# Block-sparse attention and SwiGLU: batch 1 moves from dense attention to attention by blocks

## The chip, the core and the metric

The kernel runs on one core of a Trainium2 chip. The metric is the device time of one execution in microseconds (us). The engines of the core are written as the profile writes them: PE is the matrix engine (PEld its weight loads), DVE the vector engine, ACT the scalar engine, POOL the GpSimd engine, and SP the engine that here only issues DMAs. A DMA can be issued from the queue of SP, ACT or POOL; the profile writes SPq, ACTq and POOLq for such a queue. PSUM is the memory that PE writes, in eight banks; SBUF is the memory that all engines read and write.

## What is computed

Four batches of attention with eight heads, 768 tokens and 64 elements per head, then a feed-forward part over the 3072 rows of 512 elements that come out. Tokens lie in 24 blocks of 32. A block of queries sees its own block and the two beside it, the first and the last block, and three sampled blocks; the first and the last block see everything.

```python
    scores = scale * np.matmul(q, k.transpose(0, 1, 3, 2))
    mask = np.abs(blk_i - blk_j) <= window
    mask = mask | (blk_i == 0) | (blk_j == 0) | (blk_i == n_blocks - 1) | (blk_j == n_blocks - 1)
    for qb in range(n_blocks):
        for kb in sampled_blocks[qb]:
            mask[qb * block:(qb + 1) * block, kb * block:(kb + 1) * block] = True
    scores = np.where(mask, scores, -1000000000.0)
    attn = softmax(scores)                      # written out in the reference
    x = np.matmul(attn, v)                      # (B, H, S, D) -> rows (B * S, H * D)
    xn = x / np.sqrt(np.mean(x * x, axis=-1, keepdims=True) + 1e-06) * rms_g
    g = xn @ w_gate
    out = (g / (1 + np.exp(-g)) * (xn @ w_val)) @ w_out
```

## The kernel before

**Units.** The work is cut into units (`UNITS`): a batch, the tiles of 128 tokens that the unit takes, and how many they are (1 to 3). A unit is attention for its tiles, a normalization, and the feed-forward part for them. Batch 0 has units of 1, 1, 1 and 3 tiles, batches 1 to 3 two units of 3 tiles each.

**Dense batches (0 and 1; `NDB = 2`).** Scores are computed for all pairs of tokens; the mask enters as 24 more rows of the contraction. `dk` (L322) makes scores of 128 keys by the unit's queries, `dexp` (L343) the exponentials on ACT, `dav` (L357) multiplies with the values, and `dxo` (L369, L370) divides. Tokens are dealt to partitions with a step of six (`(p c)`), so a load reads 1536 bytes in a row. Keys and queries of batch 0 are turned on PE (`tpx`, L301). Those of batch 1 are cast by `fill` into AUG and turned by a DMA transpose on SP (`turn`, L288).

**Batches by blocks (2 and 3).** Only the seen blocks are computed, four query blocks to a tile. `load_kv` and `load_q` (L452, L459) load, `fill_k`, `fill_q` and `fill_v` cast to bf16, `turn_k` and `turn_q` (L478, L504) turn keys and queries by DMA. `kg_fixed` copies the key blocks that do not depend on the data, `kg_sampled` those at sampled blocks, whose offset is in a register (both end in the helper `copy`, L144 to L148). Values are written to HBM as rows of all heads (`store_v`, L508) and gathered from there: `pair_v` (L570 to L578) what is fixed, `block_v` (L555) the sampled blocks, one DMA of 32 rows for each. `block_v` issues sampled blocks 0 and 1 from SP and block 2 from ACT. `qk` (L599), `exp` (L605), `av` (L648) and `xo` (L658, L659) do the attention; tile 5 holds the first, the last and two more blocks, whose scores are made by `qka` (L615) and `expa` (L623). Tokens are dealt in pairs (`(t p c)` with c = 2), so k and v are read 512 bytes in a row, q 256, and the turned keys hold even and odd tokens apart.

**Feed-forward.** `sq`, `rsq` and `xq` (L672 to L693) normalize. For the first six units (`NPET = 6`) xn is turned on PE (`tr`, L704) and copied out by `cp`; for the others by a DMA transpose (`xt`, L715). `proj` (L728) makes the gate part in bank 4 and the value part in bank 5, `th` (L737) takes a tanh of the gate part on ACT, `uu` (L743) and `hp` (L754) multiply on DVE. Bank 4 is free for the next gate part after `uu`. `yy` (L767) is the last matmul, `yo` (L777, L779) the copy out, `so` the store.

**Order.** No engine's order is written by hand. Every step is an `op` with the engines that may do it, an estimated duration, the steps it waits for, a priority, and the buffers or banks it takes and gives back. The loop at the end of the kernel takes, again and again, the step that can start earliest by these estimates, with priority as the tie-break, and records it; so the estimates and due times (`at`, such as `IXAT` and `RGAT`) set the order in which each engine's queue is filled. On the chip each queue runs in that order. First loads have an order of their own (`seq`). `gate_sync` is a small DMA from a loaded weight on SP, which makes the loads after it wait until that part of the weights has come.

**Registers.** The sampled blocks are read into registers by `table_regs` (L435), on POOL for key offsets and on SP and ACT for value offsets.

Of the kernel before, what the change touches and what calls it, by code (L numbers as in the profile page):

```python
# [16 lines left out]
def kernel(  # L17
# [32 lines left out]
    NR, NHP, NXN, NYO, NPET = NRND, 2, 2, 3, 6  # L50
    NSLOT, NAUG, NOPEN, NDB = 5, 2, 2, 2
    IXAT, RGAT = 36.0, 48.0
    NPT, NPA, NKG, NVG, NRAW = 4, 2, 2, 3, 3
    AHEAD, HURRY, HURU = 0.8, ("av", "xo", "sq", "rsq", "xq", "tr", "cp"), 0
# [3 lines left out]
    HD = NC * D // 2  # L58
    UNITS = [(0, 0, 1), (0, 1, 1), (0, 2, 1), (0, 3, 3)]
    UNITS += [(b, c, 3) for b in range(1, NDB) for c in (0, 3)]  # L60
    ND = len(UNITS)
    for b in range(NDB, B):
        UNITS += [(b, (5, 0, 1), 3), (b, (2, 3, 4), 3)]
    NU = len(UNITS)
    HG = [("h", 0 if u < 3 else u) for u in range(NU)]
    HO = [u if u < 3 else 0 for u in range(NU)]
# [9 lines left out]
    def bank16(n):  # L76
# [12 lines left out]
    VAC = const.tile([P, 2, H * NC, D + 2], BF16, name="VAC")  # L89
    VGC = const.tile([P, 6, VW], BF16, name="VGC")  # L90
# [6 lines left out]
    RAWD = list(A)  # L97
    RAWS = [RAWC[:, i * RB:(i + 1) * RB] for i in range(NRAW)]
    aug = [AUG[:, i] for i in range(NAUG)]
    va_ = [VAC[:, i] for i in range(2)]  # L100
    vfl = [t.rearrange("p m d -> p (m d)")[:, 0:6 * VW] for t in va_]
    VAUG = [t.rearrange("p (t c h d) -> p t c h d", t=NC // 2, c=2, h=H) for t in (vfl[0], PTC[:, 10240:10240 + 6 * VW])]
    rt_ = RAWC[:, NRAW * RB:].bitcast(BF16)
    VGB = [VGC, rt_[:, 0:6 * VW].rearrange("p (x w) -> p x w", w=VW),
           vfl[1].rearrange("p (x w) -> p x w", w=VW)]
    PD = [PTC[:, i * PDW:(i + 1) * PDW] for i in range(3)]
    PTB = [t.rearrange("p (h l x) -> p h l x", h=2, l=2) for t in [rt_[:, 6 * VW:6 * VW + 1024]] + [
        PTC[:, i * 1024:(i + 1) * 1024] for i in range(NPT - 1)]]
    PAB = [PTC[:, 3072 + i * 2048:3072 + (i + 1) * 2048].rearrange("p (l h x) -> p l h x", l=2, h=2) for i in range(NPA)]
    KTB = [t.rearrange("p (a s) -> p a s", a=NP) for t in (xs_[3], xs_[1])]  # L110
    QTB = [t.rearrange("p (a s) -> p a s", a=NP) for t in (xs_[4], PTC[:, 7168:7168 + NP * S])]
    KGB = [xs_[i].rearrange("p (x a s j c) -> p x a s j c", x=6, a=NP, s=4, j=16) for i in (0, 2)]
    KROW = AUG[:, 0].rearrange("p i e c x -> p (i e c x)").rearrange(
        "p (a c t x) -> p a c t x", a=NP, c=2, t=NC // 2)
    QROW = AUG[:, 1].rearrange("p i e c x -> p (i e c x)").rearrange("p (a n x) -> p a n x", a=NP, n=NC)
    kvv = [t.rearrange("b h (t p c) d -> b p (h t) (c d)", p=P, c=2) for t in (k, v)]
    qvv = q.rearrange("b h (n p) d -> b n p h d", p=P)
# [32 lines left out]
    zt = const.tile([P, VW], BF16, name="zt")  # L150
# [36 lines left out]
    nc.gpsimd.memset(zt[0:32, P:VW], 0.0)  # L187
# [9 lines left out]
    for t in va_:  # L197
        nc.vector.memset(t[:, :, D:D + 1], 1.0)
# [72 lines left out]
    def load(g, i):  # L271
        b, pr = divmod(g, NP)
        if i == 0:
            rawd[g] = RAWD[held["rawd", g][1]]
        nc.sync.dma_start(out=rawd[g][:, i], in_=(kv, qv, vv)[i][b, :, 2 * pr:2 * pr + 2, :])

    def fill(g, i, eng):
        copy(eng, aug[g % NAUG][:, i, :, :, 0:D],
             rawd[g][:, i].rearrange("p h (c d) -> p h c d", d=D))

    def pad_v(g, eng):
        b, pr = divmod(g, NP)
        src = rawd.pop(g) if b else A[g]
        copy(eng, va_[b][:, 2 * pr * NC:2 * (pr + 1) * NC, 0:D],
             src[:, 2].rearrange("p h (c d) -> p (h c) d", d=D))

    def turn(g):
        nc.sync.dma_start_transpose(  # L288
            out=X[g % NSLOT].rearrange("p i e (c t) -> p (i e c) t", t=P),
            in_=aug[g % NAUG].rearrange("p i e c r -> p (i e c r)"))  # L290

    def zero_pad(i):
        nc.vector.memset(aug[i][:, :, :, :, KQ:P], 0.0)
# [15 lines left out]
    held, rawd = {}, {}  # L309
# [38 lines left out]
    def dav(u, pr, bk):  # L348
        b, c0, nt = UNITS[u]
        pt, va = pts.pop((u, pr)), va_[b]  # L350
        o_ = PS[:, bk[0], 0:nt * 2 * (D + 1)].rearrange(
            "p (t e d) -> p t e d", t=nt, e=2)
        tiles["o", u, pr] = o_
        for t in range(nt):
            for e in range(2):
                for jt in range(NC):
                    nc.tensor.matmul(  # L357
                        out=o_[:, t, e, :], lhsT=pt[:, jt, e, t * P:(t + 1) * P],
                        rhs=va[:, (2 * pr + e) * NC + jt, 0:D + 1],
                        start=(jt == 0), stop=(jt == NC - 1))  # L360
# [14 lines left out]
    tab_, at_ = VGB[0].rearrange("p x w -> p (x w)"), [0]  # L375

    def small(n, dt, p=P):
# [7 lines left out]
    kti, vti = small(NS * 2, I32, 1), small(NS * NR, I32, 1)  # L385
    koff, voff = {}, {}

    REGS = {"POOL": [("k", 0, 16), ("k", 16, 32), ("k", 32, 2 * NS)], "SP": [("v", 0, 16), ("v", 16, 32), ("v", 32, 2 * NS)],
            "ACT": [("v", 2 * NS, 2 * NS + 11), ("v", 2 * NS + 11, 3 * NS)]}
    HALF = 1024  # L390

    def load_table():
        nc.sync.dma_start(
            out=stab.rearrange("p n r i -> p (n r i)"), in_=s64.rearrange("n x -> (n x)").unsqueeze(0))
        for b in range(NDB, B):
            for lo in (0, S + 32):
                nc.sync.dma_start(out=vrows[b][lo:lo + 32, :], in_=zt[0:32, :])

    def table(i, eng):
# [3 lines left out]
        elif i == 1:  # L403
            TC(out=sf, in_=stab[:, 1:NB - 1, :, 0])
            TS(out=d2, in0=sf, scalar1=16.0, scalar2=None, op0=ALU.mult)
# [17 lines left out]
        else:  # L423
# [4 lines left out]
            TS(out=vti.rearrange("p (r n) -> p n r", r=NR), in0=d2, scalar1=32.0, scalar2=32.0, op0=ALU.mult, op1=ALU.add)  # L428
# [3 lines left out]
    def table_regs(eng, part):  # L432
        e = {"POOL": nc.gpsimd, "ACT": nc.scalar, "SP": nc.sync}[eng]
        w, lo, hi = REGS[eng][part]
        _, got_ = nc.values_load_multi_w_load_instructions(  # L435
            {"k": kti, "v": vti}[w][0:1, lo:hi], engines=[e.engine], min_val=0,
            max_val={"k": 16 * (NB - 1) * (HALF + 1), "v": 32 * (NB + 1)}[w], skip_runtime_bounds_check_because=WHY)
        for i_, x in enumerate(got_):
            r, n = divmod(lo + i_, NS)
            {"k": koff, "v": voff}[w][n * NR + r] = x  # L440

    def k_at(n, r):
        x = koff[n * NR + min(r, 1)]
        if r:
            x = x >> 10 if r == 2 else x & (HALF - 1)
        return nc.s_assert_within(x, 0, 16 * (NB - 1), skip_runtime_bounds_check_because=WHY)


    def load_kv(b, i, hf):
        key = ("kv"[i], b, hf)  # L450
        raws[key] = RAWS[held["raw", key][1]]
        nc.sync.dma_start(  # L452
            out=raws[key].rearrange("p (x y) -> p x y", y=2 * D),
            in_=kvv[i][b, :, 3 * HH * hf:3 * HH * (hf + 1), :])

    def load_q(b, n):
        key = ("q", b, n // 3)
        raws[key] = RAWS[held["raw", key][1]]
        nc.sync.dma_start(  # L459
            out=raws[key][:, n % 3 * DM:(n % 3 + 1) * DM].rearrange("p (h d) -> p h d", h=H), in_=qvv[b, n])  # L460

    def fill_k(b, hf, c, eng):
        src = raws["k", b, hf].rearrange("p (a e t c d) -> p a e t c d", a=NP // 2, e=2, t=NC // 2, c=2)
        dst = KROW[:, NP // 2 * hf:NP // 2 * (hf + 1)].rearrange("p a c t (e d) -> p a c t e d", e=2)
        copy(eng, dst[:, :, c].rearrange("p a t e d -> p a e t d"), src[:, :, :, :, c, :])

    def fill_v(b, hf, c, eng):
        src = raws["v", b, hf].rearrange("p (h t c d) -> p h t c d", h=HH, t=NC // 2, c=2)
        vaugs[b] = VAUG[held["va", b][1]]
        copy(eng, vaugs[b][:, :, c, HH * hf:HH * (hf + 1), 0:D].rearrange("p t h d -> p h t d"), src[:, :, :, c, :])  # L470

    def fill_q(b, i, eng):
        copy(eng, QROW[:, :, 3 * i:3 * i + 3, :].rearrange("p a n x -> p n a x"),
             raws["q", b, i].rearrange("p (n a x) -> p n a x", n=3, a=NP))

    def turn_k(b):
        KTs[b] = KTB[held["KT", b][1]]
        nc.sync.dma_start_transpose(  # L478
            out=KTs[b].rearrange("p a (n x) -> p (a n) x", x=P), in_=KROW.rearrange("p a c t x -> p (a c t x)"))

    def tpk(b, pr, bk):
        t_ = bank16(bk[0])[:, 0:S].rearrange("p (c t x) -> p c t x", c=2, x=P)
        tiles["tk", b, pr] = t_
        for c in range(2):
            for t in range(NC // 2):
                nc.tensor.transpose(out=t_[:, c, t, :], in_=KROW[:, pr, c, t, :], identity=ident)

    def evk(b, pr, eng):
        KTs[b] = KTB[held["KT", b][1]]
        copy(eng, KTs[b][:, pr, :], tiles.pop(("tk", b, pr)).rearrange("p c t x -> p (c t x)"))  # L490

    def tpq(b, n, bk):
        t_ = bank16(bk[0])[:, 0:NP * P].rearrange("p (a x) -> p a x", x=P)
        tiles["tq", b, n] = t_
        for pr in range(NP):
            nc.tensor.transpose(out=t_[:, pr, :], in_=QROW[:, pr, n, :], identity=ident)

    def evq(b, n, eng):
        QTs[b] = QTB[held["QT", b][1]]
# [447 lines left out]
    def dep0(g0, b, c0, nt, kt, g):  # L947
        if b:
            return [("turn", g0)]
# [373 lines left out]
```

## Time and profile before

| what | value |
|---|---|
| median of three runs | 307.14 us (306.61 to 308.03) |
| the profiled execution's own time | 307.95 us |
| its span, first to last instruction | 306.2 us |
| mean granted PE clock | 0.989 |
| PE busy | 284.4 us (93%) |
| DVE, ACT, POOL busy | 195.1, 175.2, 80.3 us |
| dense scores L322, 384 columns | 144 matmuls |
| dense exponentials L343 | 96 (with 4 into another tile) |
| value gathers L555 | 88 from SP, 44 from ACT |
| sampled key copies on POOL (L146) | 132 of 328 ns in the median |
| HBM read and written | 36.70 and 8.02 MB |

The profile is of one execution. A view by stretches gives the busy time of each engine between two moments. The chain that ended last starts from the last instruction and goes back, at each step, to what released it. The waits say which engine stood idle, at which line, and what ended that. PE's matmuls are pipelined, so the time of one alone (326 ns for 384 columns) is longer than the time that each adds in a run of them.

### The profile page before, as it was taken

How to read it: one execution, taken by the hardware profiler on the slowest of the kernel's cores; microseconds unless marked ns; L12 is line 12 of the kernel's file. 1: busy time of each engine (PE TensorE's matmuls, PEld its weight loads, DVE VectorE, ACT ScalarE, POOL GpSimd, SP SyncE). 2: the span in 40 equal slices, each digit the busy share in tenths (PEclk: the TensorE clock that was granted, in tenths of full speed). 3: DMA queues.
4: the chain of work that ended last, by engine and by line, in shares of the span. 5: the costliest groups of instructions: out<-in, count | busy, mean ns of one | idle time of the engine just before them, and what ended most of it. 6: DMA issues, size and time to landing. Idle time of an engine off the chain costs nothing.

```text
span 306.2 us, 9818 instructions
## 1 busy us (share of the span) xinstructions
PE 284.4 (93%) x3838; PEld 183.4 (60%) x3838; DVE 195.1 (64%) x462; ACT 175.2 (57%) x290; POOL 80.3 (26%) x196
## 2 busy tenths in 40 slices
PE   8999989889999998999779699998699999999995
PEld 7899877666666664665445345564255655546543
DVE  6688896576756755877568435767177958807700
ACT  4899874468888785368554226877065424413322
POOL 4648100010024615119754200755041000100000
PEclk9999999999999999999999979999989999999999
DMA  7999999864799996783987973333754400060032
GB/s 218 364 242 157 203 268 323 182 229 80 119 267 266 182 308 161 159 239 87 263 196 187 195 157 97 90 84 89 166 127 135 92 36 2 0 156 0 1 98 109
DMA packets 85204, 48.50 MB, mean 158 GB/s; under 512 B 48037, under 2 KB 81318, under 8 KB 85158
## 3 DMA queue, kind: packets, MB, share of 16 engines
q1 hardware_dynamic: 76946, 41.63, 54.7%
q0 software_dynamic: 5792, 4.72, 10.1%
q10 hardware_dynamic: 2420, 1.53, 2.0%
q8 instruction: 30, 0.49, 0.6%
q14 instruction: 16, 0.13, 0.1%
HBM read 36.70 MB, written 8.02 MB: 146 GB/s over the span
## 4 chain that ended last, share of the span: by engine, by line
PE 67%; DMA 14%; DVE 8%; issue 5%; SPq 2%; ACT 2%; ACTq 1%; DVEq 0%
PE PS L728 33%; PE PS L767 15%; PE PS L322 7%; PE PS L357 4%; DMA RAWC<-in_v_dram 4%; PE PS L648 3%; DMA XC<-AUG 2%; DMA RAWC<-in_k_dram 2%; PE PS L301 2%; DMA VGC<-vrows 2%; DVE uu L743 2%; PE PS L599 2%; DMA xn<-xq 1%; DVE hp L754 1%; ACT th L737 1%
## 5 line engine op out<-in xcount | busy, mean ns | idle before, releaser
L737 ACT ACTIVATE th<-PS 128x384 bf16<-128x384 f32 x96 | 46.5, 492 | 81.9 <-PE PS L728 37.5
L743 DVE SCALAR_TENSOR_TENSOR uu<-th,PS 128x384 bf16<-128x384 bf16 x96 | 52.4, 551 | 49.4 <-ACT th L737 47.1
L728 PE MATMUL PS<-xn,wg 128*128 128x384 bf16 (+1 forms) x480 | 74.3, 294 | 7.3 <-DVE uu L743 4.2
L343 ACT ACTIVATE PTC<-PS 128x768 bf16<-128x768 f32 x92 | 70.4, 815 | 14.0 <-PE PS L322 13.8
L728 PE MATMUL PS<-xn,wv 128*128 128x384 bf16 (+1 forms) x480 | 77.9, 297 | 0.1
L767 PE MATMUL PS<-wo,hp 128*128 128x512 bf16 (+1 forms) x300 | 71.4, 376 | 4.1 <-DVE uu L743 4.1
L754 DVE TENSOR_TENSOR hp<-uu,PS 128x384 bf16<-128x384 bf16 x96 | 52.0, 551 | 16.8 <-PE PS L728 14.7
L728 PEld LDWEIGHTS <-wg 128*128 128x128 bf16 x480 | 40.7, 98 | 31.4 <-issue 9.0
L146 POOL COPY XC<-XC 128x128 bf16 x132 | 39.3, 371 | 62.6 <-PE PS L599 35.7
L728 PEld LDWEIGHTS <-wv 128*128 128x128 bf16 x480 | 40.5, 98 | 23.9 <-issue 1.9
L767 PEld LDWEIGHTS <-hp 128*128 128x128 bf16 x300 | 29.0, 99 | 32.4 <-issue 6.2
L322 PE MATMUL PS<-XC 88*128 88x128 bf16 (+1 forms) x288 | 42.6, 276 | 0.6 <-ACT PTC L343 0.6
L322 PEld LDWEIGHTS <-XC 88*128 88x128 bf16 x288 | 22.2, 100 | 7.8 <-issue 0.9
L357 PE MATMUL PS<-VAC,PTC 128*128 128x65 bf16 x552 | 21.1, 193 | 0.2 <-DVE XO L370 0.2
L357 PEld LDWEIGHTS <-PTC 128*128 128x128 bf16 x552 | 20.0, 97 | 2.0 <-issue 0.3
L777 ACT ACTIVATE yo<-PS 128x512 f32<-128x512 f32 (+1 forms) x16 | 9.1, 571 | 20.2 <-PE PS L767 20.1
L146 POOL CAST AUG<-RAWC 128x768 bf16<-128x768 f32 (+3 forms) x12 | 11.6, 973 | 30.1 <-DMA RAWC<-in_k_dram 25.7
L693 DVE SCALAR_TENSOR_TENSOR xq<-XO,rs,gB 128x512 bf16<-128x512 f32 x24 | 18.5, 792 | 0.2 <-POOL rs L686 0.2
L686 POOL TENSOR_TENSOR rs<-ms,nhalf 128x1 f32<-128x1 f32 (+1 forms) x6 | 4.3, 714 | 47.8 <-DVE ms L675 47.8
L605 ACT ACTIVATE PTC<-PS 128x1024 bf16<-128x1024 f32 x15 | 15.2, 1022 | 1.6 <-PE PS L599 1.1
L648 PEld LDWEIGHTS <-PTC 128*32 128x32 bf16 x736 | 8.1, 97 | 8.7 <-issue 7.4
L599 PEld LDWEIGHTS <-XC 64*128 64x128 bf16 x480 | 7.5, 93 | 6.9 <-issue 5.8
(112 smaller groups left out, 225.1 us busy)
## 6 DMA issues: line engine op xcount, KB each, us to landing
out_dram<-yo SPq DMA_DIRECT2D x21, 256.0 KB, 2.0
RAWC<-in_k_dram SPq DMA_DIRECT2D x4, 768.0 KB, 5.7
RAWC<-in_v_dram SPq DMA_DIRECT2D x4, 768.0 KB, 10.6
RAWC<-in_q_dram SPq DMA_DIRECT2D x12, 256.0 KB, 5.3
RAWC<-in_v_dram SPq DMA_DIRECT2D x7, 384.0 KB, 6.5
RAWC<-in_k_dram SPq DMA_DIRECT2D x6, 384.0 KB, 6.6
wg<-in_moe_w_gate_dram POOLq DMA_DIRECT2D x4, 384.0 KB, 6.9
wv<-in_moe_w_val_dram POOLq DMA_DIRECT2D x4, 384.0 KB, 7.9
```

What stands on the lines that cost most here:

```text
L146: nc.gpsimd.tensor_copy(out=out, in_=in_)
L322: nc.tensor.matmul(out=s_[:, e, j * w:(j + 1) * w], lhsT=x[0:KQ, 0, e, jt * P:(jt + 1) * P], rhs=x[0:KQ, 1, e, c0 * P:c0 * P + w], start=T ...
L343: nc.scalar.activation(out=pts[u, pr][:, g * kt:(g + 1) * kt].rearrange("p j e w -> p e j w"), in_=s_[:, :, 0:kt * w].rearrange("p e (j w) ...
L357: nc.tensor.matmul(out=o_[:, t, e, :], lhsT=pt[:, jt, e, t * P:(t + 1) * P], rhs=va[:, (2 * pr + e) * NC + jt, 0:D + 1], start=(jt == 0), ...
L605: nc.scalar.activation(out=t_.rearrange("p h l x -> p (h l x)"), in_=tiles.pop(("s", b, n, pp)).rearrange("p h l x -> p (h l x)"), func=AF ...
L648: nc.tensor.matmul(out=o_[32 * i:32 * i + 32, a, :], lhsT=l_, rhs=r_, start=i not in begun, stop=k_ == last[i], tile_position=(0, 32 * i), ...
L693: nc.vector.scalar_tensor_tensor(out=xqs[u][:, t, :], in0=xos[u, t].rearrange("p h d -> p (h d)"), scalar=mss[u][:, t:t + 1], in1=gB, op0= ...
L728: nc.tensor.matmul(out=p_[:, j, :].rearrange("p (t w) -> p t w", w=P), lhsT=w_[:, c, f_ * P:(f_ + 1) * P], rhs=xns[u][:, :, c, :], start=( ...
L737: nc.scalar.activation(out=t_, in_=tiles["gp", u, f], func=AF.Tanh, scale=0.5)
L743: nc.vector.scalar_tensor_tensor(out=t_, in0=tiles.pop(("th", u, f)), scalar=1.0, in1=tiles.pop(("gp", u, f)), op0=ALU.add, op1=ALU.mult)
L754: nc.vector.tensor_tensor(out=hps[u][:, f * fg:(f + 1) * fg, :], in0=tiles.pop(("uu", u, f)), in1=tiles.pop(("vp", u, f)), op=ALU.mult)
L767: nc.tensor.matmul(out=tiles["yp", u, t, h], lhsT=hps[u][:, f, t * P:(t + 1) * P], rhs=wo[:, f, x], start=(f == 0), stop=(f == NF - 1))
```

## The change

Only batch 0 stays dense (`NDB = 1`); batches 1 to 3 go by blocks. The dense path's own loads, casts, DMA transposes and padding for batch 1 (`load`, `fill`, `turn`, `zero_pad`) are removed. In the block batches tokens keep their natural order, so that keys, values and queries are read in rows of 64 floats, and q is loaded and cast by the functions of k (`load_kv`, `fill_k`) in two halves. Batch 1 has units of 1, 2, 1 and 2 tiles, batch 2 of 1, 2 and 3, batch 3 of 3 and 3. Of the sampled value blocks, block 0 is now issued from SP and blocks 1 and 2 from ACT; two offsets are packed into one register. The fixed key copies go to DVE alone, and casts to the engines in `CE`. Twelve units instead of six turn xn on PE. Buffers are laid out anew: four value-gather buffers instead of three, five for exponentials.

The diff, cut to its core:

```diff
-    NR, NHP, NXN, NYO, NPET = NRND, 2, 2, 3, 6
-    NSLOT, NAUG, NOPEN, NDB = 5, 2, 2, 2
-    IXAT, RGAT = 36.0, 48.0
-    NPT, NPA, NKG, NVG, NRAW = 4, 2, 2, 3, 3
-    AHEAD, HURRY, HURU = 0.8, ("av", "xo", "sq", "rsq", "xq", "tr", "cp"), 0
+    NR, NHP, NXN, NYO, NPET = NRND, 2, 2, 3, 12
+    NSLOT, NAUG, NOPEN, NDB = 5, 2, 2, 1
+    IXAT, RGAT = 44.0, 60.0
+    NPT, NKG, NVG, NRAW = 5, 2, 4, 3
+    AHEAD, HURRY, HURU = 0.4, ("av", "xo", "sq", "rsq", "xq", "tr", "cp"), 0
...
+    SPLIT = (((5,), (0,1), (2,),( 3, 4)), ((5,), (0, 1), (2, 3, 4)), ((5, 0, 1), (2, 3, 4)))
     UNITS = [(0, 0, 1), (0, 1, 1), (0, 2, 1), (0, 3, 3)]
-    UNITS += [(b, c, 3) for b in range(1, NDB) for c in (0, 3)]
     ND = len(UNITS)
     for b in range(NDB, B):
-        UNITS += [(b, (5, 0, 1), 3), (b, (2, 3, 4), 3)]
+        UNITS += [(b, ns, len(ns)) for ns in SPLIT[b - NDB]]
...
-    kvv = [t.rearrange("b h (t p c) d -> b p (h t) (c d)", p=P, c=2) for t in (k, v)]
-    qvv = q.rearrange("b h (n p) d -> b n p h d", p=P)
+    kvv = [t.rearrange("b h (t p) d -> b p (h t) d", p=P) for t in (k, v, q)]
...
-    def turn(g):
-        nc.sync.dma_start_transpose(
-            out=X[g % NSLOT].rearrange("p i e (c t) -> p (i e c) t", t=P),
-            in_=aug[g % NAUG].rearrange("p i e c r -> p (i e c r)"))
...
-    REGS = {"POOL": [("k", 0, 16), ("k", 16, 32), ("k", 32, 2 * NS)], "SP": [("v", 0, 16), ("v", 16, 32), ("v", 32, 2 * NS)],
-            "ACT": [("v", 2 * NS, 2 * NS + 11), ("v", 2 * NS + 11, 3 * NS)]}
+    REGS = {"POOL": [("k", 0, 16), ("k", 16, 32), ("k", 32, 2 * NS)],
+            "DVE": [("k", 0, 16), ("k", 16, 32), ("k", 32, 2 * NS)], "ACT": [("v", 0, 11), ("v", 11, NS)],
+            "SP": [("w", 0, NS // 2)]}
...
+    def piece(x, hi, top):
+        return nc.s_assert_within(x >> 10 if hi else x & (HALF - 1), 0, top, skip_runtime_bounds_check_because=WHY)
...
+    def v_at(n, r):
+        return piece(*((regs["SP", "w", n % (NS // 2)], n >= NS // 2) if r == 0 else (regs["ACT", "v", n], r == 2)), 32 * (NB + 1))
...
+    def fill_k(b, x, hf, c, eng):
+        src = raws[x, b, hf].rearrange("p (a e t d) -> p a e t d", a=NP // 2, e=2, t=NC)
+        dst = (KROW if x == "k" else QROW)[:, NP // 2 * hf + c].rearrange("p t (e d) -> p e t d", e=2)
+        copy(eng, dst, src[:, c])
...
-    def block_v(b, n, x, r):
-        (nc.scalar if r == 2 else nc.sync).dma_start(
-            out=new_vg(b, n)[32 * r:32 * r + 32, x, :],
-            in_=vrows[b][bass.ds(voff[(blocks(n)[x] - 1) * NR + r], 32), :])
+    def block_v(g, n, x, r):
+        (nc.scalar if r else nc.sync).dma_start(
+            out=new_vg(g, n)[32 * r:32 * r + 32, x, :],
+            in_=vrows[g][bass.ds(v_at(blocks(n)[x] - 1, r), 32), :])
...
-    CE = {2: {"POOL": 1.0}, 3: {"DVE": 0.62, "ACT": 0.86, "POOL": 1.0}}
-    QE = {2: {"POOL": 1.5}, 3: {"DVE": 1.4, "ACT": 1.47, "POOL": 1.5}}
+    CPV, CPK, KFP, KDP = 1,1,2,2
+    D_, A_, P_ = {"DVE": 0.62}, {"ACT": 0.86}, {"POOL": 1.0}
+    CE = {1: (DP_, DP_, DP_), 2: (P_,D_,D_), 3: (P_,AP_,AP_)}
+    KFE, SQE, YOE = ("DVE",), ("DVE", "ACT"), ("DVE", "ACT")
...
-        if i >= NWC - 1:
-            seq += [("ld", NP + i - NWC + 1, j) for j in range(3)]
-    seq += [("ld", g, i) for g in range(2 * NP - 1, NDB * NP) for i in range(3)]
+        if i == NWC - 1:
+            first = [("l", x, NDB, hf) for x in ORD for hf in range(2)]
+            at_ = first.index(WOG) + 1 if WOG else 0
+            seq += first[:at_]
+    seq += first[at_:]
+    seq += [("l", x, b, hf) for b in range(NDB + 1, B) for x in ORD for hf in range(2)]
...
+                gate = 2 + hf if b == NDB and i == 0 else None
+                def lkv(e, p, a=(b, i, hf), gate=gate):
+                    if gate:
+                        gate_sync(gate)
+                    load_kv(*a)
...
-            for x in xs:
-                op(("gv",) + T + (x,), {"SP": 2 * GVC}, [("st", b)] + rgs["SP", "v"], (GVP, order, x),
-                   lambda e, p, a=T + (x,): [block_v(*a, r) for r in range(2)], [("vg", T)], d=0.2)
-            for x in xs[::2]:
-                op(("gw",) + T + (x,), {"ACT": 2 * GVC}, [("st", b)] + rgs["ACT", "v"], (GWP, order, x),
-                   lambda e, p, a=T, x=x: [block_v(*a, x_, 2) for x_ in (x, x + 1)], [("vg", T)])
+                for x in xs[::2]:
+                    op(("gv",) + G + (x,), {"SP": 2 * GVC}, sts + rgs["SP", "w"], (GVP, order, x),
+                       lambda e, p, a=G, x=x: [block_v(*a, x_, 0) for x_ in (x, x + 1)], [("vg", T)], d=0.2)
+                for x in xs:
+                    op(("gw",) + G + (x,), {"ACT": 2 * GVC}, sts + rgs["ACT", "v"], (GWP, order, x),
+                       lambda e, p, a=G + (x,): [block_v(*a, r) for r in (1, 2)], [("vg", T)])
```

## The prediction

> **What bounds the kernel now.** I read the engine shares first, then the busy time by stretch, the chain that ended last (for prices), the waits, and ACT's timeline.
>
> ```profile
> PE 284.4 (93%) x3838; PEld 183.4 (60%) x3838; DVE 195.1 (64%) x462; ACT 175.2 (57%) x290; POOL 80.3 (26%) x196
> 0.00:60.00 60.00, 55.96 (x889) 49.20 (x890) 44.04 (x139) 43.72 (x66) 18.80 (x38) 1.00 1.08 245
> 60.00:120.00 60.00, 59.09 (x603) 38.56 (x601) 40.53 (x86) 46.31 (x69) 13.87 (x22) 1.00 0.94 209
> 120.00:180.00 60.00, 51.24 (x784) 29.49 (x783) 39.27 (x85) 30.20 (x52) 27.06 (x71) 0.97 0.78 186
> 180.00:240.00 60.00, 55.09 (x1093) 31.20 (x1092) 37.01 (x85) 33.84 (x60) 19.50 (x64) 0.97 0.42 107
> 240.00:306.00 66.00, 62.97 (x479) 34.97 (x477) 34.27 (x70) 21.11 (x43) 1.11 (x2) 1.00 0.20 55
> ```
>
> PE bounds the program. The stretches (columns: length, then busy PE, PEld, DVE, ACT, POOL, granted clock, DMA share, GB/s) say where it does not: 60 to 120 us, where batch 1's dense attention lies between projections, PE is busy 59.09 of 60; in 120 to 240, where batches 2 and 3 run by blocks, it is idle 8.8 + 4.9 = 13.7 us. From 240 on there is only the feed-forward part.
>
> ```profile
> 82.52 0.65 PE PS L322 x4
> 99.14 1.14 PE PS L357 x36
> 195.54 0.61 PE PS L615 x36
> 205.88 0.83 PE PS L648 x64
> 222.65 0.55 PE PS L599 x24
> 275.04 15.60 PE PS L728 x96
> 28.97 0.67 PE PS L728 x12
> 70.03 0.75 PE PS L704 x12
> ```
>
> These links of the chain (start, us, what, how many) are runs of back-to-back matmuls, so they give the price of one without its pipeline: 162.5 ns for a dense score of 384 columns (L322), 31.7 for a dense value matmul (L357), 17 and 23 for block scores (L615, L599), 13 for a block value matmul (L648), 162.5 and 56 for a projection of 384 and of 128 columns (L728), 62.5 for a transpose of xn (L704).
>
> ```profile
> ACT th L737 <- DMA VAC<-vrows: 13.4, 2, 10.6
> ACT th L737 <- DMA VGC<-vrows: 6.0, 2, 3.5
> PE PS L728 <- DMA xn<-xq: 3.1, 1, 3.1
> ```
>
> ```profile
> 168.81 0.48 ACT L737 ACTIVATE th<-PS 128x384 bf16<-128x384 f32 x1
> 169.28 5.66 ACTq L555 DMA_DIRECT2D VAC<-vrows  x3
> 175.04 0.87 ACT L737 ACTIVATE th<-PS 128x384 bf16<-128x384 f32 x2 [5.75 <-DMA XC<-AUG]
> ```
>
> The waits and ACT's timeline show one cause of that idle time: value gathers (L555) are issued from ACT's own queue between its tanh instructions (L737). Here three of them hold ACT 5.66 us, because in the built program a DMA waits for the eighth DMA before it, on SP or ACT, and that was a DMA transpose. Until the tanh is done the projection's bank is not free, and PE stops.
>
> **The change, part by part.** All sums are against the profiled execution, 307.95 us (span 306.2 and 1.75 around it), 0.8 above the median of the runs, 307.14.
>
> *Dense batch 1 leaves PE.* 96 dense scores x 0.1625 = 15.6 and 288 value matmuls x 0.0317 = 9.1: -24.7 us, on a PE 98% busy there, so on the path. Its 48 exponentials (815 ns), casts and four DMA transposes leave engines that were not the bound: 0 by themselves.
>
> *Batch 1 by blocks enters PE.* 240 scores x 0.023 = 5.5, 72 of tile 5 x 0.017 = 1.2, 448 value matmuls x 0.013 = 5.8: +12.5.
>
> *xn turned on PE* for twelve units instead of six (all but the last): 9 tiles more x 4 transposes x 0.0625 = +2.25. Three of four DMA transposes go, and with them PE's wait of 3.1 (xn<-xq): -3.1. What is late next there is the copy out of PSUM (L144, 1.44 for three tiles), between other projections. The last unit keeps its transpose.
>
> *Unit widths.* Four 3-tile, three 2-tile and six 1-tile units replace seven and three. A unit has 96 projections; 256 columns are not in the trace, between 2/3 of 162.5 (108) and twice 56 (112). New 4x96x0.1625 + 3x96x0.110 + 6x96x0.056 = 126.4 (125.9 to 127.0) against 125.3: +1.1.
>
> *One more batch of blocks brings its idle time.* 13.7 us in 120 to 240, less the 3.1 above, is 10.6 over two batches: +5.3. Below it could be 0, as in 60 to 120, or less, since all three batches' fixed key copies leave ACT (11.5 us now: 16 of 477 ns, 6 of 759) for DVE, which is at 62 to 65% there. Above it could be what ACT's queue costs, worked out as the first rival. I take 5.3, the row of the same work.
>
> *Batch 1's loads.* v is now loaded as soon as batch 0's buffers are free (its casts end at 16.5) while the weights come in; before, the first load of batch 1 waited for the third weight quarter (32.3). If weights lose what they share, wg's last quarter, which lands at 36.2 (issued 27.6, slowest landing 8.6) and is first used at 37.9, is late: 0 at the least, 10.6 at the most (the landing of a 768 KB v load). The page's rate row has 157 and 203 GB/s in the slices from 23 to 38 us against 364 in the second, so there is room: +1. [...]
>
> *Pieces of 256 bytes.* k, v and q in natural order are read in rows of 64 floats; now k and v of a block batch in 512 and only q in 256. A 256 KB load of q lands after 5.3 us, a 768 KB load of k after 5.7, of v after 10.6: per byte q is slower, mostly by its queueing. If a load takes 10.6 instead of 5.7, batch 1's chain is k issued behind the gates at 32.3 and 36.3, landed by 47, cast (0.83), turned (6.4), first six sampled copies (2.0): 57; q waits for v's buffers, one load and one turn later: about 74. PE has batch 0's attention to about 60 and its projections (24 us for the 3-tile unit, 5 to 8 left of the others) to about 90: covered, 0; with the cover gone each us late costs one. [...]
>
> *Gathers change queue.* Per tile SP issues 4 instead of 8, ACT 8 instead of 4: ACT 132 in all against 44, SP 66 against 88. Behind each on ACT stand tanh and exponentials, for which PE waits. Cost within the 5.3, and the first rival. Offsets packed in pairs add a shift or a mask per gather (32 ns in POOL's rows). Register loads: two on ACT (4.7 each) and three on POOL as now, SP one instead of three, early: 0. SP writes six zero pads instead of four (3.2 us for four) at 11 us and is then at 15.7, before v's buffers are free: 0. POOL gets 66 more copies x 0.33 and up to twelve casts x 0.83, some 30 us on an engine busy 26%; who waits for it are the block scores, priced in the chain above.
>
> Sum: -24.7 + 12.5 + 2.25 - 3.1 + 1.1 + 5.3 + 1 = -5.65, so 302.3 profiled and **301.5** as a median.
>
> **Rivals.** *1. ACT becomes the bound of the block stage: slower.* ACT now: 175.2 busy; less 39.1 (48 exponentials), plus 14.1 (half of 28.2 block exponentials), less 11.5 is 138.7. Off that the first 60 us (43.7) and the last 66 (21.1): 73.9 in the block stage. The 44 gathers hold ACT's queue 32.3 us in its timeline, 0.73 each; bare issue is 0.39 (322 + 37 + 29 ns). So 132 cost 96 or 51, and ACT needs 170 or 125 of a stage that lasts 302.3 - 1.75 - 60 - 66 = 174.5: 97% or 72%; in 120 to 240 it is 77%. An engine in order between PE and DVE will not run at 97%; at 90% the stage is 189, +14.5: 316 as a median. It decides from 0.67 per gather, where 90% of the stage (180) that makes no gain is filled: (162 - 73.9)/132. For it: the stalls of 5.66 and 10.6. Against: these follow runs of six to ten gathers beside SP's own, the new order has mostly four between pairs of tanh, and SP issues fewer.
>
> *2. The gain is eaten: no change.* Idle time of 11 for the third batch instead of 5.3 (0.67 per gather, or weights 6 late): about 307. Half a per cent, 1.5 us, is about what a measurement of this kernel can tell from none.
>
> *3. Idle time goes nearly everywhere.* If 174.5 us run as 60 to 120 does (0.9 idle in 60), idle is 2.6 instead of 10.6 + 5.3: 13 less, 288 to 289. For it: ACT loses copies, xn waits are gone. Against: POOL's sampled copies (132 now, 328 ns) become 198 and still wait for key buffers that PE frees.
>
> **How the numbers follow.** The sum, 297 to 305.5: 0.40. Rival 3 and what lies between, 288 to 297: 0.16. Rival 2: 0.10. Rival 1, 309 to 320: 0.34. Faster 0.56, same 0.10, slower 0.34. Leaving out a tenth at each end gives 292 to 316; the likeliest case alone 297 to 305.5.
>
> **What would show it.** Right: L322 with 192 matmuls and L357 with 288, no PE wait on xn but the last unit's, PE idle near 16 us between 60 and the last block value matmul, L555 on ACT 132 times at 0.6 or less. Wrong: tanh waiting on DMAs for more than 40 us in sum and stretches where ACT's queue is never idle (rival 1); PE waiting for wg or wv before 45 us (loads); first block scores after 90 us with PE idle before them (chain).

## The result and the profile after

The changed kernel takes 334.3 us in the median of four runs (331.8 to 335.0), against 306.9 for the kernel before beside it: 1.088 times as long (95% interval 1.081 to 1.096). I had forecast 301.5 with a range up to 316, so it got slower where I said faster, and the time lies outside the range.

The profiled execution of the changed kernel has a span of 332.7 us, 26.5 more than before. First its engine shares and the row of the granted clock by fortieths, then the busy time by stretch (columns as before: length, busy PE, PEld, DVE, ACT, POOL, clock, DMA share, GB/s).

```profile
PE 282.9 (85%) x4503; PEld 196.4 (59%) x4532; DVE 209.9 (63%) x514; ACT 138.4 (42%) x221; POOL 95.7 (29%) x274
...
PEclk9999989999959999799678979999679999999999
```

```profile
0.00:60.00 60.00, 54.13 (x846) 47.73 (x849) 42.15 (x138) 42.88 (x65) 21.05 (x42) 0.97 1.08 219
60.00:120.00 60.00, 50.19 (x855) 30.99 (x860) 39.06 (x95) 21.01 (x33) 23.72 (x67) 0.94 0.83 173
120.00:180.00 60.00, 44.59 (x637) 34.31 (x640) 33.87 (x69) 17.83 (x29) 10.89 (x37) 0.86 0.74 169
180.00:240.00 60.00, 45.79 (x1000) 32.73 (x1006) 37.81 (x89) 22.63 (x36) 26.36 (x80) 0.94 0.90 182
```

PE is still the busiest engine, but it is idle 49.8 us instead of 21.8. ACT, which my first rival had as the bound, is busy in 42% of the span, and no engine is near full between 60 and 240 us. The second loss hides in PE's busy time: 24.7 us of dense work are gone, and 12.5 of blocks, 2.25 of xn and 1.1 of narrower units came in by my prices, yet busy time fell by 1.5 only, and the clock is 0.86 to 0.94 where it was 0.97 to 1.00.

What PE and ACT waited for (us in total, times, longest), and SP's queue in the stretch of batch 2 (start, how long SP was held, line):

```profile
ACT th L699 <- DMA PTC<-vrows: 28.3, 5, 11.0
...
PE PS L577 <- DMA VXC<-vrows: 7.8, 1, 7.8
ACT th L699 <- DMA VXC<-vrows: 7.5, 3, 3.3
...
PE PS L577 <- DMA XC<-AUG: 5.8, 1, 5.8
...
PE PS L577 <- DMA VXC<-AUG: 4.2, 1, 4.2
```

```profile
86.80 3.98 SPq L469 DMA_TRANSPOSE VXC<-AUG  x1
...
104.26 3.43 SPq L447 DMA_DIRECT2D RAWC<-in_v_dram  x2
110.40 2.04 SPq L447 DMA_DIRECT2D RAWC<-in_k_dram  x1
...
127.77 0.40 SPq L447 DMA_DIRECT2D RAWC<-in_k_dram  x1
129.10 1.77 SPq L473 DMA_DIRECT2D vrows<-PTC  x1
134.25 3.39 SPq L447 DMA_DIRECT2D RAWC<-in_q_dram  x2
...
151.38 3.78 SPq L464 DMA_TRANSPOSE XC<-AUG  x1
...
168.09 4.68 SPq L469 DMA_TRANSPOSE XC<-AUG  x1
...
178.54 2.83 SPq L447 DMA_DIRECT2D RAWC<-in_v_dram  x2
...
233.86 3.94 SPq L469 DMA_TRANSPOSE VXC<-AUG  x1
```

L577 is the first block score of a batch (tile 5): PE waits there for the DMA transposes of each of the three batches (the 7.8 that the view puts down to a gather is the wait that ends at 240.7 us; batch 3's turn of q was issued at 233.9, and where the trace has the landing of such a turn it came 6.6 us after the issue). These three waits are 17.8 of the 49.8 us. SP's queue shows why the turns are late: from the first load of batch 2's v at 104.3 to its turn of q at 168.1 lie 64 us. The queue was held for 44 of them. Pair copies and gathers of batch 1 stand between the loads: v's casts end at 118.7, and the second k load, which takes a buffer that v leaves, goes out at 127.8 behind them. The turns of q of the three batches are issued at 86.8, 168.1 and 233.9: 81.3 and 65.8 us apart. At the prices of my forecast a block batch gives PE about 61 us of work (a quarter of the projections 31.6 and of the output matmuls 15.5, at the 0.65 us for three that the chain of before shows, blocks 12.5, xn 1.5). PE runs dry once per batch. The 81.3 and 65.8 are not the price of the transfers alone: PE's own waits lie in them, and SP waits for PE in turn (10.1 us at the pair copies, L532 and L534). Before, SP's queue held this:

```profile
107.80 5.51 SPq L452 DMA_DIRECT2D RAWC<-in_v_dram  x2
...
126.38 3.65 SPq L504 DMA_TRANSPOSE XC<-AUG  x1
...
173.77 4.45 SPq L504 DMA_TRANSPOSE PTC<-AUG  x1
```

Batch 2's turn of q went out at 126.4, after a stretch (60 to 120 us) in which batch 1's dense attention and projections kept PE 98% busy. Batch 3's followed only 47.4 us later; its v loads had gone out at 107.8, ahead of batch 2's turn of q. In the changed kernel batch 3's first load (178.5) comes behind batch 2's turn of q (168.1).

The slow clock in PE's timeline (start, us, what): the same eight projections of 256 columns, right after the wait from 168.9 to 174.7 and at 209.6.

```profile
175.66 1.89 PE L690 MATMUL PS<-xn,wv 128*128 128x256 bf16 x8
...
209.63 1.05 PE L690 MATMUL PS<-xn,wv 128*128 128x256 bf16 x8
```

### The profile page after: what moved, and what is told of

The parts are those of the page before. It is cut to its first block, busy times and chain, and to the rows that moved or that the text cites. A ratio compares the mean times of both kernels' runs of the same rounds, so it can differ in the third digit from the quotient of the medians.

```text
span 332.7 us, 11639 instructions
## 1 busy us (share of the span) xinstructions
PE 282.9 (85%) x4503; PEld 196.4 (59%) x4532; DVE 209.9 (63%) x514; ACT 138.4 (42%) x221; POOL 95.7 (29%) x274
## 4 chain that ended last, share of the span: by engine, by line
PE 60%; DMA 22%; DVE 7%; SPq 5%; issue 4%; POOL 1%; ACT 1%; POOLq 0%; ACTq 0%; DVEq 0%
PE PS L690 30%; PE PS L729 15%; PE PS L610 5%; DMA wv<-in_moe_w_val_dram 4%; DMA XC<-AUG 4%; DMA PTC<-vrows 4%; DMA RAWC<-in_k_dram 4%; PE PS L561 3%; PE PS L305 2%; DMA VXC<-vrows 2%; DMA VXC<-AUG 2%; DMA RAWC<-in_q_dram 2%; PE PS L340 2%; PE PS L577 2%; SPq L469 1%
## 5 line engine op out<-in xcount | busy, mean ns | idle before, releaser
L699 ACT ACTIVATE th<-PS 128x384 bf16<-128x384 f32 (+1 forms) x90 | 45.7, 512 | 114.0 <-PE PS L690 67.4
L690 PE MATMUL PS<-xn,wv 128*128 128x128 bf16 (+2 forms) x624 | 81.4, 275 | 7.7 <-DVE hp L716 6.5
L690 PE MATMUL PS<-xn,wg 128*128 128x128 bf16 (+2 forms) x624 | 78.9, 274 | 8.8 <-DVE uu L705 4.9
L716 DVE TENSOR_TENSOR hp<-uu,PS 128x384 bf16<-128x384 bf16 (+1 forms) x90 | 51.4, 577 | 42.3 <-PE PS L690 41.0
L150 POOL COPY XC<-XC 128x128 bf16 x198 | 51.7, 310 | 71.3 <-PE PS L577 47.4
L705 DVE SCALAR_TENSOR_TENSOR uu<-th,PS 128x384 bf16<-128x384 bf16 (+1 forms) x90 | 51.6, 577 | 26.0 <-ACT th L699 24.1
L326 ACT ACTIVATE PTC<-PS 128x768 bf16<-128x768 f32 x44 | 33.1, 817 | 7.3 <-PE PS L305 7.3
L305 PE MATMUL PS<-XC 88*128 88x128 bf16 (+1 forms) x192 | 21.8, 251 | 0.2 <-ACT PTC L326 0.2
L741 DVE TENSOR_SCALAR yo<-PS 128x512 f32<-128x512 f32 (+1 forms) x20 | 13.0, 659 | 12.5 <-PE PS L729 9.6
L152 DVE COPY XC<-XC 128x256 bf16<-128x256 bf16 (+1 forms) x63 | 16.2, 300 | 7.0 <-DMA XC<-AUG 7.0
L610 PEld LDWEIGHTS <-PTC 128*32 128x32 bf16 x1056 | 11.5, 97 | 10.9 <-issue 8.9
L577 PEld LDWEIGHTS <-XC 64*128 64x128 bf16 x216 | 5.0, 110 | 20.6 <-issue 20.3
L621 DVE TENSOR_TENSOR XO<-PS,rz 128x256 f32<-128x256 f32 x36 | 15.3, 424 | 1.2
L305 PEld LDWEIGHTS <-XC 88*128 88x128 bf16 x192 | 13.5, 100 | 2.7 <-issue 0.7
L577 PE MATMUL PS<-VXC,XC 64*128 64x64 bf16 (+1 forms) x144 | 4.0, 211 | 12.0 <-DMA VXC<-vrows 7.8
## 6 DMA issues: line engine op xcount, KB each, us to landing
PTC<-vrows ACTq DMA_DIRECT2D x68, 32.5 KB, 2.6
VXC<-vrows ACTq DMA_DIRECT2D x64, 32.5 KB, 3.2
```

What stands on the lines that cost most here:

```text
L150: nc.gpsimd.tensor_copy(out=out, in_=in_)
L152: nc.vector.tensor_copy(out=out, in_=in_)
L305: nc.tensor.matmul(out=s_[:, e, j * w:(j + 1) * w], lhsT=x[0:KQ, 0, e, jt * P:(jt + 1) * P], rhs=x[0:KQ, 1, e, c0 * P:c0 * P + w], start=T ...
L326: nc.scalar.activation(out=pts[u, pr][:, g * kt:(g + 1) * kt].rearrange("p j e w -> p e j w"), in_=s_[:, :, 0:kt * w].rearrange("p e (j w) ...
L610: nc.tensor.matmul(out=o_[32 * i:32 * i + 32, a, :], lhsT=l_, rhs=r_, start=i not in begun, stop=k_ == last[i], tile_position=(0, 32 * i), ...
L690: nc.tensor.matmul(out=p_[:, j, :].rearrange("p (t w) -> p t w", w=P), lhsT=w_[:, c, f_ * P:(f_ + 1) * P], rhs=xns[u][:, :, c, :], start=( ...
```

## The experiments

Theory A: the chain of loads, casts, turns, store and gathers of each block batch comes later than the written order assumes, and PE runs dry. Theory B (my rival 1): gathers on ACT hold up tanh. Theory C: pieces of 256 bytes make loads slow. In the first four runs all engines keep the written order of the changed kernel; only what is named differs. The runs that leave gathers or loads out of the changed kernel were timed once each, the two reorderings of loads and gathers twice, the others four times or more; four runs of the changed kernel lie within 3.2 us.

**Pieces of 512 bytes.**

```diff
-kvv = [t.rearrange("b h (t p) d -> b p (h t) d", p=P) for t in (k, v, q)]
+kvv = [t.rearrange("b h (t p c) d -> b p (h t) (c d)", p=P, c=2) for t in (k, v, q)]
...
```

> All else as in the changed kernel (same order on every engine), only the loads of q, k and v of the block batches read pieces of 512 bytes instead of 256, as before the change. The tokens then come in pairs, which the rest of the kernel does not know of, so the output is another; the time is that of the same work. Theory A (each block batch's chain of load, cast, turn, store and gathers is late because every step in the written order comes later than planned; the size of the pieces is a small part): 328 to 336. Theory C (pieces of 256 bytes make the loads slow: 8 us from issue to landing against 6 to 7, some 3 loads in a row per batch): 310 to 322, loads landing in under 6 us. Theory B (tanh behind gathers on ACT): 332 to 336.

Measured: 329.3 us (1.070 of before, 1.066 to 1.074), 5.0 less than the changed kernel. Loads land hardly earlier. The DMA issues of the changed kernel and then of this run (KB each, median us from issue to landing):

```profile
RAWC<-in_v_dram SPq DMA_DIRECT2D x6, 768.0 KB, 7.9
RAWC<-in_k_dram SPq DMA_DIRECT2D x6, 768.0 KB, 8.5
RAWC<-in_q_dram SPq DMA_DIRECT2D x6, 768.0 KB, 8.1
```

```profile
RAWC<-in_v_dram SPq DMA_DIRECT2D x6, 768.0 KB, 6.4
RAWC<-in_k_dram SPq DMA_DIRECT2D x6, 768.0 KB, 9.0
RAWC<-in_q_dram SPq DMA_DIRECT2D x6, 768.0 KB, 8.1
```

Only v lands sooner. The size of the pieces is a fifth of the loss at most; theory C falls as the main cause.

This run shows something else. PE's waits at the first block scores nearly go, from 17.8 us to 1.0, and yet little is won. PE waits for the steps behind tanh instead (16.9 us for uu, 4.9 in the changed kernel), and on ACT five gathers hold the queue for 11.75 us, until a load of k has landed. First two of PE's waits in this run, then ACT's timeline:

```profile
PE PS L690 <- DVE uu L705: 16.9, 6, 7.1
...
PE PS L577 <- DMA VXC<-AUG: 1.0, 1, 1.0
```

```profile
104.90 11.75 ACTq L517 DMA_DIRECT2D VXC<-vrows  x5
116.75 1.02 ACT L567 ACTIVATE PTC<-PS 128x1024 bf16<-128x1024 f32 x1 [10.93 <-DMA RAWC<-in_k_dram]
```

So the waits at the first scores are one place where the loss shows, and not the only one.

**88 of ACT's gathers left out.**

```diff
 def block_v(g, n, x, r):
+    (r and g > NDB) or
     (nc.scalar if r else nc.sync).dma_start(
```

> The 88 gathers on ACT of batches 2 and 3 are left out (those of batch 1 stay), so the value rows of two sampled blocks are stale there; all else is in the same order. Theory B: the waits of tanh for DMAs in batches 2 and 3 (8.5, 11.0 and 3.4 us) go, and with them PE's gaps at 160 and 240 us: 308 to 318. Theory A: SP's own chain keeps the first scores of batches 2 and 3 late, 325 to 333. In between if gathers also hold SP up by way of the completion of the eighth DMA before.

Measured: 318.5, 15.8 less, half a us outside of what B said. tanh's waits for DMAs fall from 35.8 to about 5 us. But batch 2's and 3's turns of q also move, to 162.2 and 220.8. Batch 2's wait at its first score stays (5.0 us, until 168.2), and batch 3's falls from 7.8 to 0.5. So gathers are part of the load, by two ways at once, and this run doesn't tell them apart; the run after next does.

**Short loads in batches 2 and 3.**

```diff
+m = NC * HH if b == NDB else 1
-    out=raws[key]..., in_=kvv[i][b, :, NC * HH * hf:NC * HH * (hf + 1), :])
+    out=raws[key]...[:, 0:m], in_=kvv[i][b, :, NC * HH * hf:NC * HH * hf + m, :])
```

> The loads of k, v and q of batches 2 and 3 fetch 1/24 of their bytes (one piece of 256 bytes in a partition), in the same order and with the same instructions; the values are stale. Theory A with loads as the slow step, or theory C: batches 2 and 3 have first scores 10 to 20 us earlier, 300 to 318. Theory B, or theory A with queue order and gathers as the slow step: 325 to 334.

Measured: 309.3, 25.0 less. SP's turns of k and q of batch 2 in this run:

```profile
132.35 3.60 SPq L464 DMA_TRANSPOSE XC<-AUG  x1
...
150.97 3.64 SPq L469 DMA_TRANSPOSE XC<-AUG  x1
```

The turn of q is 17 us earlier for batch 2 and 30 for batch 3, and the clock is back at 0.983 over the span, while the gathers are as many and tanh's waits for them no shorter (36.3 and 3.8 us). The waits of tanh alone therefore do not make the loss; the time that the loads take makes most of it.

**The second block's gathers back on SP.** (SP also reads ACT's two tables of offsets into registers here, 4.6 us more between 68 and 75 us.)

```diff
-(nc.scalar if r else nc.sync).dma_start(
+(nc.scalar if r == 2 else nc.sync).dma_start(
...
```

> One part undone: the gathers of the second sampled block go out from SP again (SP issues 8 per tile, ACT 4, as before the change), in the planned order of the changed kernel; PE, DVE and POOL have the same order. Theory B: waits of tanh for DMAs fall from 37 to under 20 us and the time to 315 to 326. Theory A: SP, which is the queue that is late, gets 66 more DMAs at 0.45 us and turns k and q later still: 336 to 350.

Measured: 355.8 (1.162 of before, 1.157 to 1.167), 21.5 more than the changed kernel: 0.33 us for each of 66 gathers moved, or 0.26 if the register loads cost their full 4.6. Tanh's waits did halve, as B said, and it got slower, as A said. PE's waits for gathers in this run, of which the changed kernel has none of note:

```profile
PE PS L610 <- DMA VXC<-vrows: 17.5, 8, 7.4
...
PE PS L610 <- DMA PTC<-vrows: 6.6, 4, 4.7
```

So one more DMA on SP costs more here than the same DMA on ACT. Sending these gathers from ACT, which I had feared, was the better place for them here.

Next I narrowed theory A to theory D: the turn of q is what comes late, because of SP's chain. (The 70 us of PE work per batch in its first expectation were too many; worked out above it is about 61.)

**Two wide units for batch 1.**

```diff
-SPLIT = (((5,), (0,1), (2,),( 3, 4)), ...
+SPLIT = (((5, 0, 1), (2, 3, 4)), ...
```

> One part undone: batch 1's blocks go in two units of three tiles (tiles 5, 0, 1, then 2, 3, 4) instead of 1, 2, 1 and 2; all else as in the changed kernel, the order planned anew. Theory D, formed on the runs so far (SP's queue carries each block batch through a chain of v loads, k load, turn of k, q loads, turn of q that is as long as the batch's work on PE or longer: 81 and 66 us from one turn of q to the next against some 70 us of PE work): 331 to 340, since the chain is the same and the first unit is ready later. Rival W (narrow units cost PE time: its busy time for projections is 8 us above that of before): 322 to 329.

Measured: 340.4 (1.110, 1.100 to 1.119). Narrow units in batch 1 are not the cost; without them, in an order planned anew, it is somewhat slower. Those of batch 2 stayed in.

**Loads in the order k, q, v, and SP's gathers later.**

```diff
-WOG, ORD = None, "vkq"
+WOG, ORD = None, "kqv"
```

> The loads of each block batch go out in the order k, q, v instead of v, k, q; the order on all engines is planned anew. Theory D: turn of q of batches 2 and 3 before 150 and 215 us instead of 168 and 234, PE's waits for first scores gone; but v, its store and the gathers are now last, and block values may wait on them: 315 to 340. Theory B (tanh behind gathers) says nothing of turns: 330 to 340 with the same waits of tanh.

```diff
-GVC, GVP, GWP = 0.55, 0.5, 3.5
+GVC, GVP, GWP = 0.55, 2.0, 3.5
```

> SP's gathers of the first sampled block get a later rank in the written order, so that loads and turns of the next batch pass them. Theory D: turns of q of batches 2 and 3 some 10 us earlier, 315 to 328, unless block values then wait for gathers. Theory B: unchanged, 331 to 337.

Measured: 339.4 and 347.1. Both do what theory D asks: the turns of q of batches 2 and 3 go out at 141.7 and 187.4 in the first, at 148.8 and 209.7 in the second, 19 to 46 us earlier than in the changed kernel. And both are slower. In both PE now waits for gathers at the block values (L610), 11.7 us in the first and 12.5 in the second, where the changed kernel has no such wait of note; the first has one more of 12.6 there that the view puts down to no other engine. The first's row and the second's two:

```profile
PE PS L610 <- DMA PTC<-vrows: 11.7, 8, 7.4
```

```profile
PEld L610 <- DMA VXC<-vrows: 13.3, 4, 8.9
PE PS L610 <- DMA VXC<-vrows: 12.5, 2, 8.8
```

Theory D in that form falls: it isn't the turn of q by itself. Whatever is moved ahead in the queues, something else that PE needs comes late by as much or more. What these runs leave is that the DMA work of a block batch as a whole (loads, store, turns, pair copies, gathers), in the orders tried, is not done within the batch's work on PE. Two orders, each planned anew, don't show that no order would do.

**PE kept busy in the gaps.**

```diff
 s_ = tiles["sa", b, pr] = PS[:, bk[0]:bk[0] + 2]
+[idle(1, bk[z % 2]) for z in range(64 if pr == 0 else 0)]
```

> 64 matmuls of zeros by zeros (128 columns, about 0.06 us each, into the bank that the scores then overwrite) stand ahead of the first block score of each block batch; every other instruction and its order is that of the changed kernel. They add 11.5 us of PE work, all of it where PE waits 4 to 8 us for the turn of q. If the low granted clock after such a wait (0.66 to 0.79) is a cost of its own: clock in 90 to 100, 170 to 180 and 240 to 250 us up to 0.9 or more, time 326 to 332. If it is only a sign of idle time: 333 to 338.

Measured: 337.7 (1.098, 1.088 to 1.108, against 1.081 to 1.096 of the changed kernel). Three stretches of the changed kernel, and the same three here:

```profile
90.00:100.00 10.00, 6.52 (x78) 3.53 (x79) 1.04 (x3) 3.94 (x5) 0.00 (x0) 0.66 0.62 159
170.00:180.00 10.00, 5.31 (x86) 4.05 (x86) 1.58 (x3) 3.27 (x4) 0.00 (x0) 0.66 0.72 156
240.00:250.00 10.00, 9.12 (x154) 5.20 (x155) 2.97 (x7) 4.97 (x7) 1.85 (x8) 0.69 0.46 132
```

```profile
90.00:100.00 10.00, 9.84 (x209) 7.31 (x210) 3.46 (x9) 5.66 (x7) 2.06 (x9) 1.00 0.67 160
170.00:180.00 10.00, 6.40 (x94) 5.39 (x92) 0.83 (x2) 1.94 (x2) 0.00 (x0) 0.72 0.70 154
240.00:250.00 10.00, 6.36 (x69) 3.38 (x70) 1.11 (x2) 2.74 (x4) 0.00 (x0) 0.66 0.67 173
```

The clock rose in one of three stretches: 64 such matmuls didn't fill the other gaps. No time was won. Whether the slow clock costs time beyond the idle time that it follows is not settled by this run.

**Two parts of the change alone, in the kernel before.** xn of three more units turned on PE, and the second block's gathers sent from ACT (44 moved):

```diff
-NR, NHP, NXN, NYO, NPET = NRND, 2, 2, 3, 6
+NR, NHP, NXN, NYO, NPET = NRND, 2, 2, 3, 9
```

> One part of the change alone, in the kernel before: xn of three more units is turned on PE instead of by a DMA transpose (nine units of ten; planned anew). My prediction's terms: 9 tiles x 4 transposes x 0.0625 = +2.25, PE's wait of 3.1 us for xn gone, and one DMA less of those that hold up gathers: 304 to 307. If the wait was hidden by something else that is as late: 307 to 310.

```diff
-(nc.scalar if r == 2 else nc.sync).dma_start(
+(nc.scalar if r else nc.sync).dma_start(
...
```

> One part of the change alone, in the kernel before: the gathers of the second sampled block go out from ACT instead of SP (ACT 88 in all, SP 44), in the same order of everything else. Theory B: tanh waits for DMAs 20 us longer, 313 to 322. Theory D: SP gets free 44 x 0.33 us earlier (the price of a moved gather in the changed kernel: 21.5 us for 66), tanh waits some us more, PE is the bound in most stretches: 302 to 311.

Measured: 1.0025 (0.998 to 1.007) and 1.0038 (1.0003 to 1.0073). Neither makes it faster; the second costs at most 2.2 us. In the first PE's wait for xn is gone and 2.25 us of transposes are added, by my prices -0.85 together, and nothing is won (-0.6 to +2.2). It is missing from the second's profile too, where xn is turned as before, so it hangs on the timing of the other queues. In the second, tanh's waits for DMAs stay below those of before (its longest are 3.4 and 4.0 us, against 10.6).

**Most of the block batches' DMA work left out of the changed kernel.**

```diff
+m = NC * HH if b == NDB and (i == 1 or (i, hf) == (0, 0)) else 1   # as in the short loads
+g > NDB or (nc.scalar if r else nc.sync).dma_start(                # gathers of batch 1 alone
```

> The changed kernel with most of the block batches' DMA work left out, all orders kept: k's second half and q of batch 1 and all loads of batches 2 and 3 fetch one piece of 256 bytes in a partition, and the gathers of sampled blocks of batches 2 and 3 (44 on SP, 88 on ACT) are not issued, so these values are stale. Theory D: what is left is PE's work (266 us at the prices of before) and about what of idle time the kernel before has (22): 283 to 293. If units of one and two tiles, POOL's copies of keys or DVE hold PE up: over 298.

Measured: 295.0, 39.3 less; two above what D said and under the 298 of the other case. PE's shares, then three stretches:

```profile
PE 272.5 (93%) x4532; PEld 190.1 (65%) x4532; DVE 209.1 (71%) x514; ACT 137.6 (47%) x221; POOL 97.6 (33%) x274
```

```profile
60.00:120.00 60.00, 51.72 (x940) 32.90 (x939) 40.23 (x100) 20.10 (x34) 24.51 (x72) 0.97 0.59 144
120.00:180.00 60.00, 57.45 (x1148) 44.30 (x1145) 47.95 (x107) 28.69 (x45) 27.68 (x80) 1.00 0.45 111
180.00:240.00 60.00, 59.95 (x1220) 38.60 (x1202) 46.95 (x109) 33.10 (x54) 23.13 (x79) 1.00 0.36 80
```

PE does the same matmuls in 272.5 us instead of 282.9, at a clock of 0.985, and is idle 20.8 instead of 49.8. From 120 on it is nearly full; turns of q are 62.0 and 47.9 us apart. DVE, POOL and ACT do all their work in these 295 us, so none of them was the bound.

**Short loads in the kernel before.**

```diff
+m = 1
-    in_=kvv[i][b, :, 3 * HH * hf:3 * HH * (hf + 1), :])
+    in_=kvv[i][b, :, 3 * HH * hf:3 * HH * hf + m, :])   # and one head of eight of q
```

> The counterpart of short loads in the kernel before: the loads of k, v and q of batches 2 and 3 fetch 1/24 of their bytes for k and v and 1/8 for q, in the same order; the values are stale. Theory D: there batch 1's dense attention covers batch 2's chain and only part of batch 3's is seen, so it takes 3 to 8 us off (299 to 304), against 25 in the changed kernel. If loads cost the same wherever a block batch has them: 280 to 287.

Measured: 302.1 (0.986 of before, 0.979 to 0.994), 4.9 less. The same loads that are worth 25.0 us in the changed kernel are worth 4.9 in the kernel before. The same loads are covered in the one kernel and not in the other.

## Why the prediction was wrong

**The step that failed** is "One more batch of blocks brings its idle time ... I take 5.3, the row of the same work". The row was of the same work, but not in the same place. The 10.6 us over batches 2 and 3 were measured where batch 1's dense attention lay ahead of them, and it gave PE work under which batch 2's loads, casts and turns ran. The change takes that cover away from batch 2 and adds a third chain. The runs with short loads, 25.0 us here and 4.9 in the kernel before, show that the loads were mostly hidden there and are not here. My own rule in the section on 256-byte pieces, "with the cover gone each us late costs one", was worked out for batch 1's chain alone (first scores forecast from 74 us on, under work until 90; they came at 93.5, after a wait of 4.2), and never for batches 2 and 3.

The difference of the two spans, 26.5 us, adds up from three parts:

| part | forecast | measured | from |
|---|---|---|---|
| PE's work | -8.85 (-24.7 + 12.5 + 2.25 + 1.1) | -11.9 | PE busy 284.4 before, 272.5 with DMA work left out |
| slower PE | not priced | +10.4 | PE busy 282.9 against 272.5 for the same matmuls |
| PE idle | +3.2 (5.3 + 1 - 3.1) | +28.0 | 21.8 before, 49.8 after |

So the gain on PE was there, and 3 us larger than forecast, by the run with DMA work left out. Idle time and slower matmuls, 38.4 us together, took back more than three times as much. Both all but go in that run (idle 20.8, clock 0.985), so it is the DMA work that brings them. How much of the 10.4 lies on the path is not shown.

Point by point:

- *Dense out, blocks in, xn, unit widths*: right in sum. L305 has 192 matmuls and L340 288, as forecast; wide units in batch 1 were no better (340.4).
- *xn's wait, -3.1*: the wait went, but with the 2.25 of transposes it was worth nothing in the kernel before (1.0025). In that run PE waits 2.8 us for a gather (L648), a wait of which the kernel before shows 0.6.
- *Early v loads, +1*: PE is busy 1.8 us less in the first 60 us, with waits for wg (2.0) and wv (1.2). Right in kind, and small. The weights did land later (wg after 9.9 us in the median instead of 6.9, wv 11.7 instead of 7.9), and the 1.8 lies near the +1 that I took from the rate row.
- *Pieces of 256 bytes, 0*: 5.0. Landings of v, k and q took 7.9, 8.5 and 8.1 us in the median, against 6.4, 9.0 and 8.1 with 512 bytes.
- *Gathers on ACT*: 132 of them, 0.60 us each in ACT's timeline (79 us), as forecast (0.6 or less), and below the 0.67 at which rival 1 was to decide. Tanh waited 35.8 us for DMAs, just under the 40 that I had named. In the kernel before it was 27.1 already (13.4, 6.0, 5.8 and 1.9), of which I had shown two rows. The longest wait of the changed kernel:

```profile
224.52 9.41 ACTq L517 DMA_DIRECT2D PTC<-vrows  x12
...
234.03 0.49 ACT L699 ACTIVATE th<-PS 128x384 bf16<-128x384 f32 x1 [11.02 <-DMA PTC<-vrows]
```

- *Rival 1* had the right side and named gathers, but the wrong bound: ACT is busy 138.4 us and its queue held 79 of 333; the 90% at which it counted ACT as full was taken and not measured. Its 316 would be missed by 18, and gathers back on SP cost 21.5. That leaving 88 gathers out is worth 15.8, near the +14.5 of this rival, is no sign for its bound, which was never reached.
- *"Wrong: first block scores after 90 us with PE idle before them"*: this sign, at 93.5 after 4.2 us, came true and pointed to the chain, and I gave it no rival of its own. Batch 1's wait is the smallest part of it: it stays at 4.4 us with short loads in batches 2 and 3.

What stays open: how the loss splits between the time in which a load is under way, the order of loads and gathers in SP's queue, and the wait of a DMA in the built program for the eighth before it (in the trace of before, the gather that goes out on ACT at 174.10 was held until the transpose issued on SP at 167.34 had landed, the eighth DMA before it on the two queues). The runs show what loads and gathers are worth (25.0 and 15.8, together with more gathers and loads 39.3), not the way in which each holds the queue. A rival is untested: the change also lays out buffers, load order and casts anew, and no run kept batch 1 dense with all of that. That the loads cost more here because the cover is gone, and not because of this new order, is therefore argued and not shown.

## What to carry to other kernels

Before taking work off the engine that bounds, ask what ran hidden under it: an idle time read from a stage holds only with the work that stood ahead of that stage. For each batch, set the time from its first load to the first instruction that uses it beside the work that the bound engine has in that time, and look whether the next batch's loads can start before the last batch's are used (in the kernel before they did, 47.4 us from turn to turn; here they didn't, 66 to 81 against 61 us of work). When two reorderings that bring the late step forward both make it slower, try fewer or shorter transfers before a third order: short loads gave 25.0 us here.

## What the runs showed of the hardware

- After PE's waits of 4.2, 5.8 and 7.8 us the granted clock was 0.66 to 0.69 over the 10 us slice that holds the wait's end (0.79 after one of 5.1), and eight projections of 256 columns took 1.89 us instead of 1.05. The kernel before has no wait of PE above 3.1 us. After its two longest, 3.0 us until 176.6 and 3.1 until 220.1, the clock was 0.84 and 0.83 over the 10 us slices from 170 and from 216, and it was 0.97 or more in every 60 us stretch. These are two profiles, and no run set the length of a wait: what makes the clock fall, and after how long a wait, is not shown.
- A gather of 32.5 KB moved from ACT's queue to SP's cost at most 0.33 us of the kernel's time (66 moved). The same move the other way round in the kernel before (44 moved) won nothing: 1.0038 of its time (1.0003 to 1.0073).
- Loads of 768 KB in pieces of 256 and of 512 bytes landed after about the same time (7.9, 8.5 and 8.1 us against 6.4, 9.0 and 8.1 in the median) while gathers and transposes were under way.
